# Two chunks in one TensorE group from chunk 6 instead of chunk 8, with every instruction put in order anew

## The chip, the cores and the metric

The program runs on one core of a Trainium2 chip. The core has five engines with queues of their own: TensorE (PE in the profile, with its weight loads apart as PEld), VectorE (DVE), ScalarE (ACT), GpSimd (POOL) and SyncE (SP, which issues most DMAs here). The metric is the device time of one execution in microseconds.

## The reference, cut to what matters

```
for t in range(S):                       # S = 768, B = 4, H = 8, D = 48
    state = alpha[t] * state + outer(k[t], v[t])      # per batch and head, D x D
    y[t]  = q[t] @ state
x = y as B*S tokens of H*D = 384
h = x @ w_in                             # 384 -> 2048, fp64 weights on the host
g = h * tanh(softplus(h))
out = g @ w_out                          # 2048 -> 384
```

A gated linear recurrence ("the attention") runs over 768 steps, and a feed-forward network ("the FFN") is applied to each of the 3072 tokens it gives.

## The kernel before, in words

**Chunks.** The 768 steps are cut into 12 stretches of 64. A chunk is one stretch of two of the four batches with all heads, 128 tokens, so there are 24, numbered 0 to 23; chunk n needs the state that chunk n-2 leaves. For a chunk VectorE makes two scans of the decays (`scan_rest` L672, `scan_front` L685), multiplies k and q by them (L681, L695) and decays the state (L700). TensorE then has three groups of many small matmuls: `turn` (the keys transposed, L724), `front` (what the old state gives, L752, and the scores, L763), and `back` (the scores times v, L790, and the update of the state, L802). Between front and back VectorE masks the scores; after back ScalarE takes the upper half of the fp32 result for x (`upper`, L831) and VectorE the lower half (`lower`, L837), and the state is gathered (L874).

**Two chunks in one group.** From chunk `PAIR_FROM` = 8 on, `attention` takes two chunks (two pairs of batches, same stretch of time) into one turn, one front and one back (L536 to 580). Such a pair borrows both PSUM banks `h` of the FFN for its scores and again for its update, so an FFN unit that would hold a bank then copies it away first (`put_by`, L1041, in units named by `leave_early`). Earlier chunks have their three groups each.

**Options of an unpaired chunk.** `DIRECT` chunks put their last heads straight into place with extra small matmuls (L745, L783); the others write them to a side tile x3, which six small DMAs carry into x (`move`, L858, from SP or, by `MOVER`, from ScalarE's queue). `X_PE` chunks have the lower half made by TensorE (`off`, L844) and ScalarE, with the state's update as a group of its own behind it. `STATE_PE` chunks have the old state added by TensorE (L809) in place of VectorE.

**FFN.** A unit is one of 16 blocks of 128 hidden columns for two or four chunks: nine up matmuls (L1017), seven ScalarE and VectorE steps, and three down matmuls for each chunk (L1089). 100 units run in the order of `SEGMENTS`: first four blocks for chunks 0 and 1, four for 2 and 3, then blocks 4 to 10 for chunks 0 to 3, then (unit 15 on) chunks 4 to 7, and from unit 36 on four chunks at a time. The fp64 weights of a block are loaded (L415), turned into fp32 words by three VectorE steps (L428, L433, L438), and split into an upper half by ScalarE (L449) and a lower half; `W_LOW` says which engine makes that: TensorE (L467, L468 and a copy by ScalarE), GpSimd (L477, two steps) or VectorE (L455).

**Order.** The kernel does not rely on the order of its code: `Plan.add` collects tasks with a cost, a due key, needs and buffers, and `Plan.order` simulates the engines once at build time and writes each engine's queue. Constants such as `LEAD`, `DUE_SHIFT`, `W_SHIFT`, `KEYS`, `COST` and the DMA rates feed that simulation alone. Until the model's time 43, `fill` matmuls without a result (L1165) stand where TensorE would have nothing to do.

Of the kernel before, what the change touches and what calls it, by code (L numbers as in the profile page):

```python
# [39 lines left out]
QKA = 2 * NSEG * L + NSEG * (L + 1) + 1  # L40
# [13 lines left out]
LEAD = 5.5  # L54
SPREAD = 3.0
W_LEAD = 4.25
GATE = -2.0
Q_LEAD = 4.75
V_LEAD = 9.75
FIRST_W = -22.25  # L60
# [40 lines left out]
BEGIN = {"PE": 3.0, "DVE": 4.3, "ACT": 2.2, "POOL": 4.2, "SP": 1.2}  # L101
# [20 lines left out]
class Plan:  # L122
# [26 lines left out]
    def order(self):  # L149
# [51 lines left out]
        while len(done) < n:  # L201
# [49 lines left out]
            if t.size:  # L251
                dma_free = max(at + DMA_FIRST, dma_free) + t.size / DMA_RATE
                t.late = dma_free + DMA_LAST - at
                loads.append(t)
# [20 lines left out]
KEYS = 60.0  # L275
PER_KEY = {'PE': 0.03, 'DVE': 0.02, 'ACT': 0.02, 'POOL': 0.02, 'SP': 0}
# [1186 lines left out]
```

## Time and profile before

| | us |
|---|---|
| three runs, median (lowest to highest) | 499.86 (497.8 to 502.82) |
| profiled execution, its time | 497.71 |
| its span, first to last instruction | 496.0 |
| busy in it: PE, DVE, ACT, POOL | 484.6, 323.1, 382.1, 25.3 |
| mean granted share of TensorE's clock | 0.998 |

A busy PE says that some matmul was under way, so it includes the fills. In the merged rows of a timeline the duration of a group ends with its last matmul's modelled end, which overlaps the next group; what a group costs TensorE is the difference between its start and the start of the next one. On VectorE too the recorded spans overlap a little, so starts are compared where they stand side by side.

### The profile page before, as it was taken

The numbers are of one execution on the slowest core, as the hardware profiler recorded it, in microseconds if no ns is written. First come the engines' busy times: TensorE is split into PE (matmuls) and PEld (weight loads), VectorE is DVE, ScalarE is ACT, GpSimd is POOL, SyncE is SP. The second block draws the span as 40 slices with busy tenths as digits, with TensorE's granted clock in tenths as the row PEclk, the third lists the DMA queues.
The fourth block names the chain that finished last, engine by engine and source line by source line (L and its number), as shares of the span: only waits on it lengthen the run. The fifth ranks groups of instructions, "written<-read, shape, count | busy, mean of one in ns | idle before, by whom it ended". The sixth has DMA issues, their size and how long they took to land.

```text
span 496.0 us, 12822 instructions
## 1 busy us (share of the span) xinstructions
PE 484.6 (98%) x5319; PEld 432.5 (87%) x5319; DVE 323.1 (65%) x522; ACT 382.1 (77%) x864; POOL 25.3 (5%) x27
## 2 busy tenths in 40 slices
PE   6999999999999999999999999999999999999995
PEld 4688889899899989999989899999989899999994
DVE  7999999999973694447867783863474343343333
ACT  3578786886788778857777897889789899997772
POOL 2003201413000000000000000000000000000000
PEclk9999999999999999999999999999999999999999
DMA  7877544606000250115152543603153412100001
GB/s 248 316 285 236 181 151 157 238 35 214 13 0 9 78 172 1 66 59 175 28 213 75 183 164 99 207 24 118 71 171 93 172 41 106 64 1 0 1 0 68
DMA packets 18926, 56.22 MB, mean 113 GB/s; under 512 B 3440, under 2 KB 11312, under 8 KB 18864
## 3 DMA queue, kind: packets, MB, share of 16 engines
q1 hardware_dynamic: 18592, 55.11, 32.5%
q8 instruction: 42, 0.69, 0.6%
q10 hardware_dynamic: 272, 0.26, 0.2%
q14 instruction: 20, 0.16, 0.1%
HBM read 48.87 MB, written 4.72 MB: 108 GB/s over the span
## 4 chain that ended last, share of the span: by engine, by line
PE 85%; DVE 9%; DMA 3%; issue 1%; ACT 1%; SPq 0%; DVEq 0%; ACTq 0%
PE sums_at L1089 39%; PE h_at L1017 37%; PE att_at L790 2%; PE att_at L752 2%; DVE w_lead L433 2%; PE h_at L763 2%; DMA ws<-in_wp_dram 1%; DVE w_lead L438 1%; PE att_at L724 1%; DMA qka<-in_qka_dram 1%; PE h_at L802 1%; DVE w_lead L428 1%; DVE t L1044 1%; DVE g L1054 1%; DVE rest L672 1%
## 5 line engine op out<-in xcount | busy, mean ns | idle before, releaser
L1089 PE MATMUL sums_at<-ws,g 128*128 128x384 f32 x1152 | 223.9, 340 | 0.1
L1017 PE MATMUL h_at<-xs,ws 128*128 128x512 f32 (+1 forms) x900 | 214.2, 384 | 0.2 <-DVE t L1044 0.2
L1089 PEld LDWEIGHTS sums_at<-ws,g 128*128 128x128 f32 x1152 | 202.4, 188 | 8.1 <-ACT ws L471 0.4
L1017 PEld LDWEIGHTS h_at<-xs,ws 128*128 128x128 f32 x900 | 163.3, 188 | 28.4 <-DVE t L1044 0.5
L1054 DVE SCALAR_TENSOR_TENSOR g<-t,g 128x512 fp32r<-128x512 f32 (+1 forms) x100 | 67.8, 679 | 124.2 <-ACT g L1051 123.9
L1026 ACT ACTIVATE t<-h_at 128x512 f32<-128x512 f32 (+1 forms) x100 | 58.0, 580 | 63.6 <-PE h_at L1017 60.8
L1051 ACT ACTIVATE g<-t 128x512 fp32r<-128x512 f32 (+1 forms) x100 | 60.3, 604 | 11.5 <-PE sums_at L1089 5.3
L1029 ACT ACTIVATE t<-t 128x512 f32<-128x512 f32 (+1 forms) x100 | 61.3, 613 | 2.3
L1032 ACT ACTIVATE t<-t 128x512 f32<-128x512 f32 (+1 forms) x100 | 61.2, 612 | 2.2
L1044 DVE SCALAR_TENSOR_TENSOR t<-t,h_at 128x512 f32<-128x512 f32 (+1 forms) x87 | 57.1, 657 | 8.3 <-ACT t L1035 8.2
L1035 ACT ACTIVATE t<-t 128x512 f32<-128x512 f32 (+1 forms) x100 | 60.4, 604 | 0.5
L672 DVE TENSOR_TENSOR_SCAN rest<-qka,behind 112x520 f32<-112x520 f32 x24 | 30.4, 1268 | 0.4 <-DMA qka<-in_qka_dram 0.2
L685 DVE TENSOR_TENSOR_SCAN qka<-qka,ahead 112x520 f32<-112x520 f32 x24 | 30.6, 1274 | 0.0
L477 POOL TENSOR_TENSOR ws<-w_lead,ws 128x384 fp32r<-128x384 f32 x14 | 22.1, 1598 | 98.3 <-ACT ws L449 98.3
L1026 ACT ACTIVATION_READ_ACCUMULATOR t<-h_at 128x1 f32 x100 | 19.4, 194 | 0.0
L1041 DVE COPY held<-h_at 128x512 f32<-128x512 f32 x13 | 9.0, 691 | 15.8 <-ACT t L1026 15.8
L831 ACT ACTIVATE xs<-att_at 112x384 fp32r<-112x384 f32 (+1 forms) x24 | 12.2, 513 | 6.2 <-PE att_at L809 3.4
L695 DVE TENSOR_TENSOR qka<-qka 112x512 f32<-112x512 f32 x24 | 16.4, 684 | 0.1
L681 DVE TENSOR_TENSOR qka<-qka,rest 112x512 f32<-112x512 f32 x24 | 15.8, 659 | 0.0
L433 DVE SCALAR_TENSOR_TENSOR w_lead<-ws,w_lead 128x768 int32<-128x768 int32 x16 | 15.7, 982 | 0.1
L438 DVE SCALAR_TENSOR_TENSOR w_lead<-ws,w_lead 128x768 int32<-128x768 int32 x16 | 15.3, 957 | 0.1
L449 ACT ACTIVATE ws<-w_lead 128x768 fp32r<-128x768 f32 x16 | 13.4, 839 | 2.3 <-DVE w_lead L438 2.2
(100 smaller groups left out, 366.7 us busy)
## 6 DMA issues: line engine op xcount, KB each, us to landing
qka<-in_qka_dram SPq DMA_DIRECT2D x22, 772.5 KB, 5.8
ws<-in_wp_dram SPq DMA_DIRECT2D x16, 768.0 KB, 4.5
wc<-in_wp_dram SPq DMA_DIRECT2D x16, 768.0 KB, 4.5
v<-in_vp_dram SPq DMA_DIRECT2D x24, 192.0 KB, 4.5
out_dram<-osb SPq DMA_DIRECT2D x15, 192.0 KB, 2.6
xs<-x SPq DMA_DIRECT2D x104, 16.0 KB, 1.8
out_dram<-part SPq DMA_DIRECT2D x8, 192.0 KB, 2.6
qka<-in_qka_dram SPq DMA_DIRECT2D x2, 260.5 KB, 4.4
```

Source lines behind the costliest of these rows:

```text
L433: nc.vector.scalar_tensor_tensor(lead.tile, words(1), -0x40000000, lead.tile, ALU.bitwise_and, ALU.bitwise_or)
L672: nc.vector.tensor_tensor_scan(t[:, :0:-1], alpha()[:, :0:-1], behind[:, ::-1], 0.0, ALU.mult, ALU.max)
L685: nc.vector.tensor_tensor_scan(a, a, ahead, 0.0, ALU.mult, ALU.max)
L1017: nc.tensor.matmul(p[:, :N].rearrange("p (c t) -> p c t", c=nt), wi[:, z, f, s], x[:, :, s, a], start=m == 0, stop=m == len(passes) - 1,)
L1026: nc.scalar.activation(wide(t), wide(h), AF.Exp, accum_out=vchk[:, at : at + 1])
L1029: nc.scalar.activation(wide(t), wide(t), AF.Square, bias=1.0)
L1032: nc.scalar.activation(wide(t), wide(t), AF.Ln, bias=0.2, scale=0.2)
L1035: nc.scalar.activation(wide(t), wide(t), AF.Exp, scale=-1.0)
L1044: nc.vector.scalar_tensor_tensor(wide(y), wide(t), 2.5, wide(held), ALU.subtract, ALU.mult)
L1051: nc.scalar.activation(g.tile[:, 0, :N], wide(y), AF.Copy, scale=-0.4, accum_out=own)
L1054: nc.vector.scalar_tensor_tensor(g.tile[:, 1, :N], wide(y), -0.4, g.tile[:, 0, :N].bitcast(F32), ALU.mult, ALU.subtract,)
L1089: nc.tensor.matmul(o.tile, g.tile[:, a, j * C : (j + 1) * C], wo[:, z, f], start=begins and m == 0, stop=end and m == 2,)
```

## The change

`PAIR_FROM` goes from 8 to 6, so chunks 6 and 7 become a pair. Beside it nearly all constants of the order are new, and some of them choose other engines: `DIRECT` loses chunks 0, 6 and 7; `X_PE` goes from {0, 1} to chunks 1 to 5 (its higher entries name paired chunks and do nothing); `STATE_PE` goes from {2, 6} to 3, 4 and 5 (6 and 7 do nothing); `W_LOW` no longer uses GpSimd: blocks 4, 7, 8, 11, 12, 13 and 15 go to VectorE, and blocks 0 and 2 use the banks `h`. The weights of the six blocks in `PARTS` are loaded and converted in two halves. One cast at the start (L333) is gone, and the last output goes out by SP's queue. The model's costs and DMA rates are new as well.

```diff
-LEAD = 5.5
+LEAD = 5.75
...
-W_LEAD = 4.25
+W_LEAD = 6.75
...
-Q_LEAD = 4.75
-V_LEAD = 9.75
-FIRST_W = -22.25
+Q_LEAD = 6.5
+V_LEAD = 6.75
+FIRST_W = -20.25
...
 DUE_SHIFT = {
-    0: -3.75, 1: 1.75, 2: 2.5, 3: 1.0, 4: -1.5, 5: 2.0, 6: 2.0, 7: 2.0, 8: -4.5, 9: -6.5, 10: -11.25,
...
+    0: -5.25, 1: -5.5, 2: -4.5, 3: 1.75, 4: -1.0, 5: -0.5, 6: -3.25, 7: 4.5, 8: -1.0, 9: -7.75,
...
-X_PE = {0, 1}
+X_PE = {1, 2, 3, 4, 5, 6, 7, 8, 9}
 SIDES = 2
-STATE_PE = {2, 6}
-PAIR_FROM = 8
+STATE_PE = {3, 4, 5, 6, 7}
+PAIR_FROM = 6
 BACK_AFTER = 0.8
-DIRECT = {0, 1, 2, 3, 6, 7}
+DIRECT = {1, 2, 3}
 W_LOW = {
-    0: ('PE', 'o0'), 1: ('PE', 'o0'), 2: ('PE', 'o3'), 3: ('PE', 'o3'), 4: ('POOL', ''), 5: ('PE', 'o0'),
-    6: ('DVE', ''), 7: ('POOL', ''), 8: ('POOL', ''), 9: ('DVE', ''), 10: ('DVE', ''), 11: ('POOL', ''),
-    12: ('POOL', ''), 13: ('POOL', ''), 14: ('DVE', ''), 15: ('POOL', ''),
+    0: ('PE', 'h'), 1: ('PE', 'o0'), 2: ('PE', 'h'), 3: ('PE', 'o0'), 4: ('DVE', ''), 5: ('PE', 'o3'),
+    6: ('DVE', ''), 7: ('DVE', ''), 8: ('DVE', ''), 9: ('DVE', ''), 10: ('DVE', ''), 11: ('DVE', ''),
+    12: ('DVE', ''), 13: ('DVE', ''), 14: ('DVE', ''), 15: ('DVE', ''),
 }
...
+PARTS = {7, 8, 10, 12, 14, 15}
+OUT_LATER = 4.0
...
-FLIGHT = 1800.0
+FLIGHT = 2200.0
...
-DMA_RATE, DMA_FIRST, DMA_LAST = 285.0, 1.1, 0.9
+DMA_RATE, DMA_FIRST, DMA_LAST, DMA_EACH = 355.0, 1.7, 0.8, 0.1
+DMA_SLOW, DMA_SLOW_UNTIL = 0.3, 22.0
...
-KEYS = 60.0
-PER_KEY = {'PE': 0.03, 'DVE': 0.02, 'ACT': 0.02, 'POOL': 0.02, 'SP': 0}
+KEYS = 80.0
+PER_KEY = {'PE': 0.02, 'DVE': 0.05, 'ACT': 0.02, 'POOL': 0.08, 'SP': 0.01}
...
-    causal_f = sb.tile([P, L], F32, tag="rest", name="causal_f", bufs=BUFS["rest"])
+    causal_f = const.tile([P, L], F32, name="causal_f")
...
-    causal = const.tile([P, L], U32, name="causal")
-    nc.vector.tensor_copy(causal, causal_f)
-    causal8 = causal.unsqueeze(1).unsqueeze(1).broadcast_to([P, 2, NPAIR, L])
+    causal8 = causal_f.bitcast(U32).unsqueeze(1).unsqueeze(1).broadcast_to([P, 2, NPAIR, L])
...
     def weight(f):
         key = weight_unit[f] - W_LEAD + W_SHIFT.get(f, 0.0)
+        if f not in PARTS:
+            weight_part(f, slice(0, 2), key, "")
+            return
+        for m in range(2):
+            weight_part(f, slice(m, m + 1), key + m * OUT_LATER, "1")
+
+    def weight_part(f, which, key, part):
         stage = plan.buffer("stage")
+        size = which.stop - which.start
...
-                queue = nc.scalar if n == n_chunks - 1 else nc.sync
-                queue.dma_start(by_token[c * L : (c + 1) * L, 2 * b : 2 * b + 2], osb.tile)
+                nc.sync.dma_start(by_token[c * L : (c + 1) * L, 2 * b : 2 * b + 2], osb.tile)
```

## Rows read from the trace of the kernel before

**Rows 1.** The page's first part: busy time, share of the span and instructions.
```profile
PE 484.6 (98%) x5319; PEld 432.5 (87%) x5319; DVE 323.1 (65%) x522; ACT 382.1 (77%) x864; POOL 25.3 (5%) x27
```
**Rows 2.** Windows: stretch, PE, PEld, DVE, ACT, POOL busy, clock, DMA share, GB/s.
```profile
0.00:23.00 23.00, 17.55 (x277) 12.72 (x278) 19.80 (x31) 8.71 (x21) 3.25 (x13) 1.00 0.80 273
...
45.00:92.00 47.00, 46.99 (x778) 41.69 (x778) 46.15 (x74) 36.23 (x88) 10.82 (x7) 1.00 0.54 190
```
**Rows 3.** The first window for the fills of L1165 alone (PE, PEld).
```profile
0.00:23.00 23.00, 9.80 (x29) 5.92 (x29) 1.00 0.80 273
```
**Rows 4.** Timeline of PE, chunk 6 (unpaired): start us, us, line, count.
```profile
70.28 0.58 PE L745 MATMUL att_at<-qka,v_apart 48*64 48x64 f32 x24
...
71.59 2.35 PE L1089 MATMUL sums_at<-ws,g 128*128 128x384 f32 x12
73.87 0.58 PE L783 MATMUL att_at<-probs,v_apart 64*64 64x64 f32 x24
...
75.07 0.90 PE L809 MATMUL att_at<-state,ident 112*112 112x192 f32 x4
75.68 2.36 PE L1017 MATMUL h_at<-xs,ws 128*128 128x512 f32 x9
```
**Rows 5.** Timeline of PE, the pair of chunks 8 and 9.
```profile
112.87 0.69 PE L752 MATMUL att_at<-qka,state 48*64 48x64 f32 x32
...
114.89 1.33 PE L1089 MATMUL sums_at<-ws,g 128*128 128x384 f32 x6
...
118.11 2.26 PE L1089 MATMUL sums_at<-ws,g 128*128 128x384 f32 x12
120.29 0.69 PE L790 MATMUL att_at<-probs,v 64*64 64x64 f32 x32
...
122.11 1.33 PE L1089 MATMUL sums_at<-ws,g 128*128 128x384 f32 x6
```
**Rows 6.** The chain that ended last: start us, us; twelve downs between ups.
```profile
105.85 2.12 PE sums_at L1089 x12
```
**Rows 7.** Timeline of PE, chunk 0's lower half (`off`) and the next group.
```profile
14.35 0.51 PE L844 MATMUL att_at<-xs,minus_ident 128*128 128x192 f32 x2
14.68 0.57 PE L724 MATMUL sums_at<-ident,qka 112*128 112x112 f32 x4
```
**Rows 8.** Timelines of DVE and PE where unit 15 begins.
```profile
90.72 0.56 DVE L837 TENSOR_TENSOR xs<-att_at,xs 128x384 fp32r<-128x384 f32 x1
91.19 0.56 DVE L874 TENSOR_TENSOR state<-att_at,state 112x384 f32<-112x384 f32 x1
...
91.64 2.24 PE L1017 MATMUL h_at<-xs,ws 128*128 128x512 f32 x9
```
**Rows 9.** Line L428 until 91.2 us: count, ns min/median/max, first and last start.
```profile
L428 DVE TENSOR_SCALAR w_lead<-ws x12: 545/552/562, 8.7 to 85.8; 128x768 int32<-128x768 int32 x12
```
**Rows 10.** Groups of VectorE by line and shape: busy us, mean ns | idle before.
```profile
L433 DVE SCALAR_TENSOR_TENSOR w_lead<-ws,w_lead 128x768 int32<-128x768 int32 x16 | 15.7, 982 | 0.1
...
L1041 DVE COPY held<-h_at 128x512 f32<-128x512 f32 x13 | 9.0, 691 | 15.8 <-ACT t L1026 15.8
L837 DVE TENSOR_TENSOR x<-att_at,x 112x128 fp32r<-112x128 f32 x18 | 5.1, 283 | 1.5 <-ACT xs L831 1.4
L455 DVE TENSOR_TENSOR ws<-w_lead,ws 128x768 fp32r<-128x768 f32 x4 | 3.8, 954 | 0.0
```
**Rows 11.** Lines L477 (GpSimd) and L685 (a scan): ns min/median/max.
```profile
L477 POOL TENSOR_TENSOR ws<-w_lead,ws x14: 1012/1184/4257, 45.0 to 123.3; 128x384 fp32r<-128x384 f32 x14
L685 DVE TENSOR_TENSOR_SCAN qka<-qka,ahead x24: 1226/1233/2056, 5.7 to 370.7; 112x520 f32<-112x520 f32 x24
```
**Rows 12.** DMA issues: count, KB each, median us to landing; L858's issue ns.
```profile
out_dram<-osb SPq DMA_DIRECT2D x15, 192.0 KB, 2.6
xs<-x SPq DMA_DIRECT2D x104, 16.0 KB, 1.8
...
out_dram<-osb ACTq DMA_DIRECT2D x1, 192.0 KB, 3.2
...
L858 SPq DMA_DIRECT2D xs<-x x104: 507/587/1611, 51.3 to 406.0; - x104
```

More of the change, by code (lines that the diff above doesn't have):

```diff
@@ L251, in order @@
             if t.size:
-                dma_free = max(at + DMA_FIRST, dma_free) + t.size / DMA_RATE
+                dma_free = max(at + DMA_FIRST, dma_free) + t.size / DMA_RATE + DMA_EACH
+                dma_free += DMA_SLOW * (2.0 < at < DMA_SLOW_UNTIL and t.size > 300)
                 t.late = dma_free + DMA_LAST - at
@@ L410, in weight @@
         key = weight_unit[f] - W_LEAD + W_SHIFT.get(f, 0.0)
+        if f not in PARTS:
[4 more added lines that the diff above has]
+    def weight_part(f, which, key, part):
         stage = plan.buffer("stage")
+        size = which.stop - which.start
         def load():
-            t = new(stage, [P, 2, DM, 2], f"ws{f}", dtype=I32)
+            t = new(stage, [P, size, DM, 2], f"ws{f}", dtype=I32)
             return nc.sync.dma_start(
                 t.rearrange("p m c w -> p (m c w)"),
-                w[f].rearrange("p m c -> p (m c)").bitcast(I32),
+                w[f, :, which].rearrange("p m c -> p (m c)").bitcast(I32),
             )
-        got = add(
-            "SP", *COST["load"], max(key, FIRST_W + f) - 4, load, uses=[stage], size=786
-        )
+        first = max(key, FIRST_W + f) - 4
+        got = add("SP", *COST["load"], first, load, uses=[stage], size=393 * size)
         lead = plan.buffer("lead")
@@ L426, in begin @@
         def begin():
-            new(lead, [P, 2, DM], f"w_lead{f}", dtype=I32)
+            new(lead, [P, size, DM], f"w_lead{f}", dtype=I32)
             nc.vector.tensor_scalar(
@@ L455, in lower @@
                 nc.vector.tensor_tensor(lo, both(), hi.bitcast(F32), ALU.subtract)
-            b = add("DVE", *COST["w lo2"], key + 0.035, lower, [a], [lead], port=True)
-            ready_w[f, 0] = ready_w[f, 1] = [a, b]
+            b = add("DVE", *COST[f"w lo{size}"], key + 0.035, lower, [a], [lead], port=True)
+            for m in range(which.start, which.stop):
+                ready_w[f, m] = [a, b]
             return
-        for m in range(2):
+        for m in range(size):
             k = key + 0.5 * m
@@ L481, in weight @@
                 b = add("POOL", *COST["w lo"], k + 0.04, lower, [a], [lead], port=True)
-            ready_w[f, m] = [a, b]
+            ready_w[f, which.start + m] = [a, b]
     def weight_check(f):
@@ L654, in chunk @@
             got_a, got_k, got_q = (
-                add("SP", *COST["load"], -99 + 0.1 * i, load_part(*e), uses=[q_buf], size=230)
+                add("SP", *COST["load"], -99 + 0.1 * i, load_part(*e), uses=[q_buf], size=263)
                 for i, e in enumerate(((a_at, QKA), (k_at, a_at), (0, k_at)))
@@ L665, in chunk @@
             got_a = got_k = got_q = add(
-                "SP", *COST["load"], key - Q_LEAD, load, uses=[q_buf], size=692
+                "SP", *COST["load"], key - Q_LEAD, load, uses=[q_buf], size=791
             )
@@ L1064, in unit @@
         t_exp = add("ACT", *cost("exp"), k, exp, [t_up], [h, t])
-        t_sq = add("ACT", *cost("act"), k + 0.01, square, [t_exp], [t])
+        t_sq = add("ACT", *cost("square"), k + 0.01, square, [t_exp], [t])
         t_ln = add("ACT", *cost("ln"), k + 0.02, log, [t_sq], [t])
@@ L1151, in send @@
                 b, c = chunks[n]
[L1152 to L1153 removed]
+                nc.sync.dma_start(by_token[c * L : (c + 1) * L, 2 * b : 2 * b + 2], osb.tile)
             copied = add("ACT" if on_act else "DVE", *COST["stash"], k, copy, done, [o, osb])
[L1156 to L1157 removed]
+            add("SP", *COST["store"], k + 0.001, send, [copied], [osb])
     if FILLS:
```

57 lines of the change are left out of this document (29 added, 28 removed), and 4 rows, old and new, of the table DUE_SHIFT.

## The prediction, made before the changed kernel was seen running

> **What bounds the kernel now.** I read the busy times first. TensorE has work under way for 98% of the span, VectorE for 65% [rows 1]. That is an average over stages, so I cut the span into windows. In the first 23 us TensorE is busy for 17.55, but 9.80 of that are fills, which compute nothing [rows 2, 3]. Real work is therefore 17.55 - 9.80 = 7.75 us, and 15.25 us of TensorE's time are lost before the first FFN unit has got going. From 45 to 92 us TensorE has no gap at all (46.99 of 47) and VectorE hardly one (46.15 of 47) [rows 2]. So two engines are full there at once: VectorE prepares chunks and weights, and TensorE uses them up as they come. How tight this is shows at unit 15, the first that needs chunks 4 to 7: the lower half of chunk 7's x starts on VectorE at 90.72, the next instruction there starts at 91.19, and the unit's first up matmul starts at 91.64 [rows 8]. After that the chain of waits is TensorE's own work, ups and twelve downs in turn (2.12 us a set of downs [rows 6]), up to the end.
>
> So the end is: TensorE's total work, plus what it loses before unit 15, plus a short tail. The change can act through these three alone, and all chunks and blocks it touches before unit 15 must also pass VectorE, which has no room. After unit 15 the work is the same in both kernels.
>
> **TensorE's work, part by part.** All durations are differences of starts.
>
> Pairing chunks 6 and 7. Unpaired, chunk 6 has a front of 71.59 - 70.28 = 1.31, and a back with update and state of 75.68 - 73.87 = 1.81, of which the state on TensorE (L809) is 75.68 - 75.07 = 0.61 [rows 4]. Chunk 7 is the same without the state, 1.31 + 1.20. Together 5.63. The pair of 8 and 9 has a front of 114.89 - 112.87 = 2.02 and a back of 122.11 - 120.29 = 1.82, together 3.84 [rows 5]. The turns have as many matmuls either way; I count them at nothing. That is -1.79. A group of small matmuls also slows the FFN group beside it: twelve downs take 2.12 undisturbed [rows 6], 73.87 - 71.59 = 2.28 between a front and a back [rows 4], and 120.29 - 118.11 = 2.18 with one such neighbour [rows 5], so some 0.08 a border. Three groups fewer are six borders, -0.47. Sum -2.3.
>
> Lower halves on TensorE. Chunk 0's `off` takes 14.68 - 14.35 = 0.33 [rows 7]. Chunks 2 and 3 gain one each. Chunks 4 and 5, which are not direct, have twice as many matmuls in it: no row shows that, so between 0.33 and 0.66; I take 0.5, since the added ones are narrower. In each of the four the update becomes a group of its own, two borders or 0.16. Together 0.66 + 1.0 + 0.64 = +2.3. Chunk 0 loses its `off` and the extra group, -0.5, and by not being direct about 0.3 more, the difference per chunk between chunk 6's back without the state (1.20) and half of the pair's (0.91) [rows 4, 5].
>
> State on TensorE. Chunks 3, 4 and 5 in place of 2 (chunk 6 is counted above): two more at 0.61 [rows 4], +1.2.
>
> The five blocks whose lower weights TensorE makes stay five. Sum: -2.3 + 2.3 - 0.8 + 1.2 = **+0.4 us**. What the pair saves on TensorE is spent on taking work from VectorE.
>
> **VectorE before unit 15.** Removed: the large x step, 0.47 by the start of its neighbour [rows 8], for chunks 2 and 3, and that with the small one (0.28 [rows 10]) for 4 and 5: -2.4. State additions, of the same size as the large x step: three go, those of chunks 2 and 6 come, -0.5. Added: both x steps for chunk 0, +0.75; the small step for 6 and 7, +0.6; one or two copies that clear the borrowed banks, 0.69 each at most [rows 10], +1.1; lower weights of blocks 4, 7 and 8, 0.95 each [rows 10], +2.8. Halving the steps of blocks 7, 8 and 10: not in the trace; from nothing up to 0.1 for each of twelve steps that become two, I take +0.7. Given back by GpSimd: one scan took 2.06 against a median of 1.23 [rows 11]; the others that met GpSimd's steps before unit 15 lost little, so -1.0. The removed cast gives nothing, as VectorE is idle for 3.2 of the first 23 us anyway [rows 2], most of it before data is there. Sum **+2.1 us**. The cover: until 91.2 VectorE had begun 12 blocks' conversions [rows 9], and only eleven are needed before unit 25. The twelfth can wait, 0.55 + two times 0.98 or 2.5 us [rows 9, 10]. So I cost VectorE's surplus at nothing; without that cover unit 15 comes up to 2.1 us later.
>
> Here the Trainium skill speaks for more. SBUF — State Buffer, "Who interferes with whom", says that VectorE with two SBUF inputs and GpSimd reading SBUF share one read interface, and that the second "fully blocks" until the first is done. By that page all 10.82 us of GpSimd's work from 45 to 92 [rows 2] could stand in VectorE's way, and the sum would be lower by up to 9. The scan's one doubling agrees with the page; the near-full VectorE and median steps of usual length do not show such a loss, so I keep 1.0.
>
> **The moves.** Chunks 0, 6 and 7 now send six small DMAs each. An issue takes 0.59 us and a landing 1.8 [rows 12]. Chunk 0's are hidden behind chunk 1's scans. Those of 6 and 7 stand between the pair's last x step and unit 15, where before the x step alone did: for one chunk's six on one queue 6 x 0.59 + 1.8 = 5.3 us. They hide if the pair is done that much earlier, under the downs of the units before; its due keys are earlier. Bounds 0 and 5.3; I take 0.5, because TensorE in that stretch still has units of blocks 8 to 10 to do, but no reserve beyond [rows 2]. SP's loads stand behind these moves; DMA is at 0.54 there, which is room.
>
> **The start and the tail.** What the new order does in the first 23 us no row shows. The supplier, VectorE, is idle for 23 - 19.80 = 3.2 us [rows 2], so -3.2 is as far as a fuller start goes, and I take the same for a load that comes late. Value -0.5. The last store lands in 2.6 us from SP where ScalarE's queue took 3.2 [rows 12]: between 0 and -0.6, value -0.3.
>
> **Sum.** +0.4 + 0 + 0.5 - 0.5 - 0.3 = +0.1 against the profiled execution's 497.71, or 497.8. That execution is 2.15 below the median of the runs (499.86), so the same sum against the median is 500.0. I put the forecast between them, **498.9 us**.
>
> **Rivals.**
> A, the start closes. The loads are due in another order, and GpSimd no longer touches VectorE. For it: 15.25 us lost, the largest loss there is. Against: unit 15 waits for VectorE, whose work does not shrink, so TensorE would only wait later. With -3.2 and another -2 from VectorE meeting no GpSimd: 498.9 - 5.2 = 493.7. The lock that the Trainium skill describes would act through this case.
> B, unit 15 waits, slower than before. The pair needs both chunks scanned, masked and moved, and borrows both `h` banks while VectorE is full; VectorE's +2.1 is uncovered and 3 of the 5.3 us of moves show. 498.9 + 5.1 = 504.0. It decides once the pair's last move lands after the downs of units 12 to 14 have run out.
> C, the pairing does nothing that shows: TensorE's +0.4 without the six borders (+0.47): 499.4.
>
> **How the numbers follow.** A measurement of this kernel tells about 1% (5 us) from no change. Forecast 0.60, A 0.15, B 0.15, C 0.10. A and B lie across the 1% bound with two thirds to three quarters of their weight: faster 0.11, same 0.77, slower 0.12. The range takes in the forecast's terms (-3.2 at the start, +2.1 and more at unit 15), the 2 us between runs and part of A and B: 494.5 to 503.5.
>
> **What would show it.** Chunks 6 and 7 as one front of about 2.0 and one back of about 1.8 us; no row of GpSimd at L477's successor; scans near 1.23 throughout; unit 15 within 3 us of 91.64; fills and gaps before 23 us between 12 and 18 us; no TensorE wait after unit 15. The prediction is wrong if unit 15 starts before 88 or after 95, or if a new wait of TensorE on VectorE or on a move appears between 60 and 100 us.

## The result, and the profile after

The changed kernel takes 505.9 us (median of 4 runs, 505.04 to 506.23) against 499.62 of the kernel before on the same chip (4 runs, 497.8 to 502.82). The ratio is **1.0139, 95% interval 1.0111 to 1.0166**: slower by 1.4%, and outside the range given. The profiled execution took 505.04 us with a span of 503.3; before it was 497.71 and 496.0, so 7.3 us are to be found.

The page of the changed kernel, first part; it answers to [rows 1]:

```profile
PE 491.3 (98%) x5267; PEld 437.2 (87%) x5267; DVE 328.0 (65%) x552; ACT 386.1 (77%) x874; POOL 3.2 (1%) x13
```

TensorE is busy for 6.7 us more, fills included, with 52 matmuls fewer. The share of the span, 98%, says nothing of it. The windows do (stretch, PE, PEld, DVE, ACT, POOL busy, clock, DMA share, GB/s); the first and the last answer to [rows 2]:

```profile
0.00:23.00 23.00, 19.64 (x261) 13.85 (x261) 18.64 (x31) 7.72 (x20) 3.21 (x13) 1.00 0.73 237
23.00:45.00 22.00, 21.03 (x403) 16.63 (x403) 21.04 (x33) 15.46 (x43) 0.00 (x0) 1.00 0.80 272
45.00:92.00 47.00, 46.96 (x726) 41.60 (x725) 44.94 (x82) 35.33 (x87) 0.00 (x0) 1.00 0.56 181
```

The second stretch of the kernel before, which [rows 2] leaves out:

```profile
23.00:45.00 22.00, 21.89 (x416) 17.82 (x414) 21.97 (x37) 17.16 (x47) 0.00 (x0) 1.00 0.76 275
```

From 45 to 92 us TensorE has no gap, as before. Ahead of 45 us its busy time holds more fills. The window from 0 to 45 us for the fills alone, first of the kernel before, then of the changed one (PE, PEld):

```profile
0.00:45.00 45.00, 10.50 (x31) 6.22 (x31) 1.00 0.78 274
```

```profile
0.00:45.00 45.00, 15.61 (x45) 9.29 (x45) 1.00 0.77 254
```

So 5.1 us more of TensorE's time there compute nothing. Fills and gaps together go from 15.25 to 16.11 us in the first 23 us, and from 0.81 to 3.83 us between 23 and 45. A ledger of TensorE's time up to the first matmul of unit 15, by differences of starts, makes this exact; here is the first matmul of unit 15 in the changed kernel, beside the one in [rows 8]:

```profile
97.33 0.86 PE L1030 MATMUL h_at<-xs,ws 128*128 128x512 f32 x3
```

| until unit 15 starts | before | changed | difference |
|---|---|---|---|
| fills | 9.90 | 14.75 | +4.85 |
| gaps | 2.73 | 1.47 | -1.26 |
| work that counts | 76.17 | 78.21 | +2.04 |
| before the first matmul | 2.85 | 2.89 | +0.04 |
| unit 15 starts at | 91.64 | 97.33 | +5.69 |

From unit 15 to unit 36 another 1.06 us are lost (97.02 against 98.08), from 36 to 99 nothing (291.20 against 291.19), and from unit 99 to the span's end 0.56 (16.14 against 16.70). 5.69 + 1.06 - 0.01 + 0.56 = 7.30.

The 1.06 us have one place. VectorE of the changed kernel, and TensorE beside it (start us, us, engine, line; in brackets the idle time before and its releaser):

```profile
184.70 1.24 DVE L685 TENSOR_TENSOR_SCAN rest<-qka,behind 112x520 f32<-112x520 f32 x1 [2.06 <-DMA qka<-in_qka_dram]
...
186.66 1.23 DVE L698 TENSOR_TENSOR_SCAN qka<-qka,ahead 112x520 f32<-112x520 f32 x1
187.81 0.66 DVE L1057 SCALAR_TENSOR_TENSOR t<-t,h_at 128x512 f32<-128x512 f32 x1
...
188.53 1.21 PE L1030 MATMUL h_at<-xs,ws 128*128 128x512 f32 x4 [1.31 <-DVE t L1057]
```

Chunk 13's load lands late, its scans stand in VectorE's queue, and the gate (L1057) that gives an h bank back to TensorE stands behind them.

What the prediction said of single steps shows up. The pair of chunks 6 and 7 on TensorE, the answer to [rows 5]: front 78.44 - 76.42 = 2.02, back 85.64 - 83.83 = 1.81 us.

```profile
76.42 0.69 PE L765 MATMUL att_at<-qka,state 48*64 48x64 f32 x32
...
78.44 1.32 PE L1102 MATMUL sums_at<-ws,g 128*128 128x384 f32 x6
...
83.83 0.69 PE L803 MATMUL att_at<-probs,v 64*64 64x64 f32 x32
...
85.64 0.63 PE L1102 MATMUL sums_at<-ws,g 128*128 128x384 f32 x2
```

And the scans, where [rows 11] had one of 2.06 us (ns min/median/max):

```profile
L698 DVE TENSOR_TENSOR_SCAN qka<-qka,ahead x24: 1215/1234/1237, 5.7 to 389.5; 112x520 f32<-112x520 f32 x24
```

### The profile page after: what moved, and what is told of

Its sections match the earlier page's. It is cut to its first block, busy times and chain, and to the rows that moved or that the text cites. A ratio compares the mean times of both kernels' runs of the same rounds, so it can differ in the third digit from the quotient of the medians.

```text
span 503.3 us, 12781 instructions
## 1 busy us (share of the span) xinstructions
PE 491.3 (98%) x5267; PEld 437.2 (87%) x5267; DVE 328.0 (65%) x552; ACT 386.1 (77%) x874; POOL 3.2 (1%) x13
## 4 chain that ended last, share of the span: by engine, by line
PE 89%; DVE 5%; DMA 4%; issue 1%; ACT 0%; SPq 0%; DVEq 0%
PE sums_at L1102 40%; PE h_at L1030 38%; DMA ws<-in_wp_dram 3%; PE att_at L765 2%; PE att_at L803 2%; PE h_at L776 2%; PE att_at L737 1%; DMA qka<-in_qka_dram 1%; PE h_at L815 1%; DVE qka L698 1%; DVE w_lead L444 1%; DVE rest L685 1%; PE sums_at L480 1%; PE att_at L822 0%; DVE w_lead L449 0%
## 5 line engine op out<-in xcount | busy, mean ns | idle before, releaser
L1057 DVE SCALAR_TENSOR_TENSOR t<-t,h_at 128x512 f32<-128x512 f32 (+1 forms) x84 | 55.0, 654 | 9.8 <-ACT t L1048 9.6
L685 DVE TENSOR_TENSOR_SCAN rest<-qka,behind 112x520 f32<-112x520 f32 x24 | 29.7, 1236 | 3.8 <-DMA qka<-in_qka_dram 3.6
L461 ACT ACTIVATE ws<-w_lead 128x384 fp32r<-128x384 f32 (+1 forms) x22 | 14.6, 662 | 9.0 <-DVE w_lead L449 8.9
L1054 DVE COPY held<-h_at 128x512 f32<-128x512 f32 x16 | 11.0, 689 | 14.3 <-ACT t L1039 14.2
L1176 PE MATMUL sums_at<-minus_ident 128*128 128x512 f32 x45 | 15.6, 474 | 2.9 <-ACT minus_ident L340 2.9
L449 DVE SCALAR_TENSOR_TENSOR w_lead<-ws,w_lead 128x384 int32<-128x384 int32 (+1 forms) x22 | 16.0, 733 | 0.2
L444 DVE SCALAR_TENSOR_TENSOR w_lead<-ws,w_lead 128x384 int32<-128x384 int32 (+1 forms) x22 | 16.0, 734 | 0.2
L803 PEld LDWEIGHTS att_at<-probs,v 64*48 64x48 f32 (+1 forms) x744 | 13.0, 126 | 3.1 <-issue 1.8
L803 PE MATMUL att_at<-probs,v 64*48 64x64 f32 (+1 forms) x744 | 15.7, 220 | 0.0
## 6 DMA issues: line engine op xcount, KB each, us to landing
qka<-in_qka_dram SPq DMA_DIRECT2D x22, 772.5 KB, 5.4
```

Of the source, the lines that this page charges most:

```text
L685: nc.vector.tensor_tensor_scan(t[:, :0:-1], alpha()[:, :0:-1], behind[:, ::-1], 0.0, ALU.mult, ALU.max)
L803: nc.tensor.matmul(y[64 * a : 64 * a + wide, u, j], V()[own, h : h + wide], probs[slot][own, a, j], start=first and j == 0 and not direct ...
L1057: nc.vector.scalar_tensor_tensor(wide(y), wide(t), 2.5, wide(held), ALU.subtract, ALU.mult)
```

## The experiments

After the result I held **theory S**: the new order gives VectorE and TensorE their work ahead of 45 us so that TensorE runs short, and the rest is TensorE's own extra work. Rivals were late loads (L), VectorE's amount of work ahead of unit 15 (V), and pairing itself (P). All kernels keep the order of every queue unless it says otherwise; each ratio is to the kernel before, timed beside it. When a unit's first up matmul starts, in the profiled executions (us):

| kernel | unit 0 | unit 3 | unit 8 | unit 15 | unit 36 | unit 97 | span | ratio (95%) |
|---|---|---|---|---|---|---|---|---|
| before | 22.72 | 40.87 | 55.32 | 91.64 | 188.66 | 471.52 | 496.0 | 1 |
| changed | 29.81 | 41.95 | 63.27 | 97.33 | 195.41 | 478.25 | 503.3 | 1.0139 (1.0111 to 1.0166) |
| e1 | 29.82 | 41.02 | 62.37 | 96.40 | 193.89 | 476.70 | 501.8 | 1.0106 (1.0088 to 1.0124) |
| e2 | 29.62 | 41.10 | 62.35 | 96.41 | 194.43 | 477.23 | 502.2 | 1.0116 (1.0101 to 1.0131) |
| e3 | 29.25 | 40.69 | 62.47 | 96.54 | 198.19 | 481.04 | 505.5 | 1.0202 (1.0183 to 1.0220) |
| e4 | 28.71 | 40.16 | 61.48 | 95.55 | 194.20 | 477.00 | 501.9 | 1.0112 (1.0086 to 1.0138) |
| e5 | 28.78 | 40.77 | 62.60 | 96.60 | 194.86 | 477.70 | 502.7 | 1.0148 (1.0128 to 1.0168) |
| e6 | 30.20 | 41.42 | 62.76 | 96.81 | 193.88 | 476.69 | 501.8 | 1.0071 (1.0051 to 1.0091) |
| g1 | 29.49 | 40.54 | 61.86 | 96.11 | 194.18 | 477.01 | 502.0 | 1.0100 (1.0073 to 1.0126) |
| g2 | 28.96 | 40.14 | 62.15 | 96.91 | 194.54 | 477.35 | 502.5 | 1.0136 (1.0109 to 1.0163) |
| k1 | 29.58 | 40.77 | 62.16 | 95.58 | 193.94 | 476.75 | 501.8 | 1.0093 (1.0072 to 1.0114) |
| j1 | 23.74 | 41.85 | 63.17 | 97.24 | 195.42 | 478.28 | 503.6 | 1.0111 (1.0090 to 1.0131) |
| h1 | 29.23 | 41.53 | 63.18 | 97.21 | 194.70 | 477.50 | 503.0 | 1.0131 (1.0110 to 1.0152) |
| h2 | 29.68 | 41.98 | 63.62 | 98.26 | 195.79 | 478.62 | 503.3 | 1.0125 (1.0105 to 1.0145) |
| h3 | 29.91 | 42.22 | 63.86 | 97.93 | 195.43 | 478.26 | 502.9 | 1.0126 (1.0108 to 1.0143) |
| b1 | 22.61 | 41.61 | 57.04 | 93.36 | 190.36 | 473.22 | 497.7 | 1.0042 (1.0025 to 1.0058) |
| f1 | 29.78 | 40.42 | 61.31 | 95.82 | 192.19 | 474.68 | 499.6 | 1.0097 (1.0072 to 1.0122) |
| f2 | 31.21 | 40.87 | 60.56 | 100.70 | 197.99 | 480.16 | 505.8 | 1.0193 (1.0170 to 1.0216) |
| f3 | 28.38 | 41.18 | 59.23 | 97.97 | 194.55 | 476.19 | 502.3 | 1.0150 (1.0108 to 1.0193) |
| f5 | 28.66 | 39.48 | 60.08 | 99.36 | 196.21 | 478.40 | 503.9 | 1.0131 (1.0105 to 1.0157) |

The changed kernel, e3, e4 and e6 are the same up to unit 32, and their unit 15 starts at 97.33, 96.54, 95.55 and 96.81. So 1.8 us at unit 15 between single profiles is no effect. The spread stands ahead of unit 3 (40.16 to 41.95); loads land at different times there, and block 0's conversion begins at 9.2, 8.6, 8.1 and 9.6 us. The time from unit 3 to unit 15 tells more: it is 55.38 to 55.40 us in the changed kernel, e1, e4, e6 and j1 (55.85 in e3). The ratios have the intervals beside them; two of them less than some 0.0035 apart can't be told from each other.

**Are the loads late? e1.**

```diff
-            if t.paced:
+            if False and t.paced:
```

> The changed kernel with the rule 'few loads in flight' taken out: every load is issued as soon as its buffer is free; order of all queues kept. Changed kernel for comparison: 505.04 us profiled, ratio 1.0139 to the kernel before. Theory S (the start's order: TensorE loses about 3 us more than before ahead of 45 us because VectorE and TensorE are given work in an order that leaves TensorE short, and the loads are only a part of it): between -1.0 and +0.5 us against the changed kernel, unit 0 still after 28 us. Rival L (late loads: blocks and chunks land too late because only two loads may be in flight): -2 to -4 us, unit 0 before 27 us and the waits of VectorE for blocks at 9.2 and 33.6 us gone.

Unit 0 starts at 29.82 and unit 15 at 96.40, within that spread. VectorE still waits for block 0's load at 9.2 us (1.16 us). Only the wait at 187 us shrinks, from 1.31 to 0.8. Theory L falls for the start.

**Does TensorE's extra work set unit 15? e2 and e5.** e2 adds the states of chunks 3 to 5 on VectorE, e5 makes the lower halves of chunks 2 to 5 there.

```diff
+STATE_DVE = {3, 4, 5}                                  # e2
-            if on_pe:
+            if on_pe and n not in STATE_DVE:           # in update, and so in gather
...
+LOWER_DVE = {2, 3, 4, 5}                               # e5: off issues nothing,
+                    nc.vector.tensor_tensor(to(1), of, to(0).bitcast(F32), ALU.subtract)   # left does this
```

> The changed kernel with the states of chunks 3, 4 and 5 added by VectorE as for most chunks before, in place of two matmuls each and a copy by ScalarE; order kept. Takes 3 x 0.61 = 1.83 us off TensorE from 44.7 us on, gives VectorE three steps of about 0.55. Theory S (from 45 us on TensorE's own work sets the time and VectorE has cover): -1.2 to -1.9 us against the changed kernel, that is 503.2 to 503.8. Rival V (the prediction's view, unit 15 waits for VectorE, which has no room): 0 to +1.6 us, unit 15 later than 97.3 us or a TensorE wait ahead of it.

> The changed kernel with the lower halves of x of chunks 2, 3, 4 and 5 made by VectorE, in place of matmuls and a copy by ScalarE; order kept. Takes 0.33 + 0.33 + 0.56 + 0.51 us off TensorE (the first two ahead of 45 us, where it is short of work anyway), gives VectorE four steps of 0.47 and two of 0.28, +2.4 us. Theory S (TensorE's own work sets the time from 45 us on, VectorE has cover): -0.7 to -1.7 us against the changed kernel. Rival V (VectorE without room sets unit 15): +0.5 to +2.4 us, with TensorE waiting for VectorE between 45 and 97 us.

Neither theory has its way: unit 15 starts at 96.41 and 96.60, as without the edits, and 55.31 and 55.83 us after unit 3. In e2 the first place where the saving is lost is a new wait of TensorE for the state that VectorE now adds:

```profile
44.84 0.55 DVE L888 TENSOR_TENSOR state<-att_at,state 112x384 f32<-112x384 f32 x1
...
45.45 0.60 PE L738 MATMUL att_at<-ident,qka 112*128 112x112 f32 x4 [0.80 <-DVE state L888]
```

So e2 could not tell whether TensorE's stream sets unit 15, since it put a step with a wait in place of what it took. k1 takes the same matmuls out and puts nothing there.

```diff
+STATE_OUT = {3, 4, 5}
-            if on_pe:
+            if on_pe and n not in STATE_OUT:
```

> The changed kernel with the two matmuls that add the old state left out for chunks 3, 4 and 5 and nothing put in their place (this part of the computation is missing; every other instruction and the order of all queues stay). It takes 3 x 0.61 = 1.83 us off TensorE, as e2 did, but without e2's new step on VectorE for which the next turn had to wait. Theory T (from 45 us on TensorE's own stream sets the time; e2 lost its gain to the wait on VectorE that it brought): unit 15 at 94.6 to 95.2 us where e1, e3 and e6 had 96.4 to 96.8, time -1.5 to -1.8 us against the changed kernel. Rival Q (something that no experiment has touched sets unit 15): 96.2 or later, time unchanged.

Unit 15 starts at 95.58, which is within the spread of the kernels with the same start (e4: 95.55), and the ratio, 1.0093, has an interval that overlaps the changed kernel's. Counted from unit 3 it comes after 54.81 us in place of 55.38 to 55.40, so 0.57 of the 1.83 us arrive; expected were 1.5 to 1.8. From unit 8 to unit 15 the 0.61 us of chunk 5's group arrive in full (33.43 against 34.04 to 34.07). Ahead of unit 8 the two other groups bring nothing (21.38 from unit 3 to unit 8, against 21.32 to 21.34): a front (L766) now waits 0.5 us at 46.7 us for ScalarE's copy of the turned keys. So theory T holds in part: TensorE's stream sets the time from unit 8 to unit 15, and ahead of that other waits stand close behind it.

**Does VectorE's amount of work set it? g1 and g2.** g1 gives the lower weights of blocks 4 and 6 to 10 to GpSimd again; g2 adds e2 and half of e5.

```diff
+LOW_POOL = {4, 6, 7, 8, 9, 10}
+                if f in LOW_POOL:
+                    for m in range(size):
+                        nc.gpsimd.tensor_tensor(
+                            lo[:, m], both()[:, m], hi[:, m].bitcast(F32), ALU.subtract
+                        )
+                    return
                 nc.vector.tensor_tensor(lo, both(), hi.bitcast(F32), ALU.subtract)
```

> The changed kernel with the lower weights of blocks 4 and 6 to 10 made by GpSimd, half a block at a time, as the kernel before did for four of them; order of all queues kept. Takes some 5 us off VectorE ahead of unit 15 and nothing off TensorE. Theory V (VectorE's work ahead of unit 15 alone sets its start): unit 15 at 92 to 94 us in place of 96.4 to 97.3, time -2 to -4 us against the changed kernel. Theory T (TensorE's own work alone sets it from 45 us on, as it has no gap there): unit 15 within 0.5 us of 96.5, time unchanged. Theory B (both engines are loaded to the same level there, and one relieved alone leaves the other): as T here, but g2 gains.

> g1, and besides the states of chunks 3 to 5 and the lower halves of x of chunks 4 and 5 on VectorE in place of TensorE: both engines relieved at once (VectorE by 5 less 3.1 us, TensorE by 1.83 + 1.07 = 2.9). Theory B: unit 15 at 94 to 95 us, time -1.5 to -2.9 us against the changed kernel, where e2 and e5 (TensorE relieved alone) left unit 15 at 96.4 and 96.6. Theory V: no better than g1. If unit 15 stays at 96.4 here too, neither engine's amount of work but a chain between them sets it (the two h banks that the pair borrows, the queue order).

The windows of g1:

```profile
0.00:23.00 23.00, 19.54 (x261) 13.93 (x261) 19.12 (x31) 7.99 (x20) 3.21 (x13) 1.00 0.73 243
23.00:45.00 22.00, 21.95 (x409) 17.65 (x410) 21.90 (x35) 16.24 (x44) 0.00 (x0) 1.00 0.77 270
45.00:97.00 52.00, 52.00 (x749) 45.90 (x748) 47.92 (x82) 40.36 (x98) 15.12 (x11) 1.00 0.53 174
```

VectorE has 4.1 us of slack from 45 to 97 us, TensorE none, and unit 15 starts at 96.11, 55.57 us after unit 3. Theory V falls: unit 15 does not wait for VectorE's amount of work. g2 gains nothing either (96.91); TensorE waits there 3.8 us in three places for states that VectorE adds, more than in e2.

**Is it unit 0's late start? j1.** Block 2's lower weights use bank o3, so that unit 0 need not wait for an h bank.

```diff
-    0: ('PE', 'h'), 1: ('PE', 'o0'), 2: ('PE', 'h'), 3: ('PE', 'o0'), ...
+    0: ('PE', 'h'), 1: ('PE', 'o0'), 2: ('PE', 'o3'), 3: ('PE', 'o0'), ...
```

> The changed kernel with block 2's lower weights worked out in bank o3 instead of an h bank; every task keeps its place in the order but for unit 0, which no longer waits for block 2 to give the h bank back. Asked: is it unit 0's late start (29.8 us against 22.7) that costs the time ahead of 45 us? If it is: units 0 to 15 all come earlier, unit 15 by 1 us or more, and fills fall by as much. If TensorE's supply as a whole is short there (blocks and chunks that come late from VectorE): unit 0 at 23 to 25 us, units 3 to 15 within 0.5 us of where they were, fewer fills early and as many more later, time within 0.5 us of the changed kernel.

```profile
23.74 1.31 PE L1198 MATMUL h_at<-xs,ws 128*128 128x256 f32 x9
...
97.24 1.09 PE L1198 MATMUL h_at<-xs,ws 128*128 128x512 f32 x4
```

Unit 0 comes 6.1 us earlier, unit 3 0.1, unit 15 0.1. The most visible difference between the two starts is a symptom: the place in TensorE's queue that unit 0 leaves is not filled by anything that comes earlier too.

**Is it the order of chunks and blocks on VectorE? h1, h2 and b1.** Up to 45 us VectorE spends 21.7 us on chunks (scans, multiplications, decays) and 16.2 on blocks' conversions before, and 22.9 and 13.8 in the changed kernel. TensorE has begun five units before (a sixth at 44.99) and four after. h1 puts two scans behind two blocks in the changed kernel, h2 does so without the rule on loads, b1 puts two scans ahead of two blocks in the kernel before.

```diff
+    behind_of(nth("chunk.<locals>.scan_rest", 4), nth("weight_part.<locals>.ends", 3))   # h1, h2
+    behind_of(nth("chunk.<locals>.scan_rest", 5), nth("weight_part.<locals>.ends", 5))
...
+    ahead_of(nth("chunk.<locals>.scan_rest", 4), nth("weight.<locals>.signs", 3))        # b1
+    ahead_of(nth("chunk.<locals>.scan_rest", 5), nth("weight.<locals>.begin", 5))
```

> The changed kernel with two steps of VectorE moved and nothing else: the first scan of chunk 4 (31.05 us) to behind block 3's conversion (it ends at 36.5), the first scan of chunk 5 (41.4 us) to behind the conversion of the sixth block (46.9), so that blocks come ahead of chunks as in the kernel before. Theory S (TensorE runs short ahead of 45 us because VectorE makes chunks ready before the blocks that the first units need): the block's conversion can begin only when its load has landed (33.4 us), so VectorE waits there and most of the gain is lost: unit 3 within 0.5 us of 41.0, unit 15 within 0.7 of 96.5, time -0.5 to +0.5. Rival (the queue order alone is enough): unit 3 before 40.2, time -1 or more.

> h1, and the rule 'few loads in flight' taken out as in e1, so that block 3's load is issued 2.4 us earlier. Theory S: now unit 3 at 39.5 to 40.3 us (e1 without the move: 41.02), fills and gaps ahead of unit 15 some 1 us less than in e1, unit 15 at 95.2 to 95.9 (e1: 96.40), time -0.5 to -1.2 us against e1 (1.0106). If unit 15 stays at 96.4 although unit 3 comes earlier, TensorE's short supply ahead of 45 us is not in these two scans.

> The kernel before with the opposite edit and nothing else: on VectorE the first scan of chunk 4 (33.5 us) goes ahead of two of the three steps of the block converted at 30.8 to 33.1 us, and the first scan of chunk 5 (45.7) ahead of the block begun at 40.9. Their loads have landed by then. Theory S: blocks come 1.2 us later, units 3 and 4 about 1.2 us later than 40.87 and 42.46, more fills ahead of 45 us, and 0.8 to 2 us more in all (ratio 1.0015 to 1.004). Rival (TensorE's supply there does not hang on the order of chunks and blocks): ratio within 0.001 of 1.

b1 has the size that theory S expects: the split up to 45 us becomes 22.9 and 14.7, units 3, 5 and 8 start 0.7, 1.2 and 1.7 us later, unit 15 at 93.36, and the ratio is 1.0042 (2.1 us). The way there is another. The moved scan stands between two steps of a block, but ahead of the lower half of chunk 2's x (L837) too:

```profile
30.78 1.24 DVE L672 TENSOR_TENSOR_SCAN rest<-qka,behind 112x520 f32<-112x520 f32 x1
31.94 0.93 DVE L433 SCALAR_TENSOR_TENSOR w_lead<-ws,w_lead 128x768 int32<-128x768 int32 x1
32.79 0.55 DVE L837 TENSOR_TENSOR xs<-att_at,xs 128x384 fp32r<-128x384 f32 x1
```

ScalarE's copy of the state waits for that step, and chunk 3's turn on TensorE waits for the copy (who waits for whom, us in total, times, longest):

```profile
PE att_at L724 <- ACT state L872: 1.0, 1, 1.0
```

Up to unit 15 gaps grow by 1.15 us and fills by 0.10. So b1 shows what the places of two steps on VectorE are worth; that it is late blocks that leave TensorE short, it does not show.

The same edit the other way round does not give it back. h1 is as expected, at the edge of its bounds; h2 misses: unit 3 at 41.98, not 39.5 to 40.3. In h2 block 3's conversion ends 1.2 us earlier than in the changed kernel, but its second half on TensorE (L480) comes at the old time, since it needs a bank that ScalarE's copy (L484) gives free, and ScalarE stands ahead of that copy for a check (L702) that reads chunk 4's scan:

```profile
38.45 0.31 ACT L702 ACTIVATE chk<-qka,minus 112x8 f32<-112x8 f32 x1 [1.38 <-DVE qka L698]
...
38.97 0.47 ACT L484 ACTIVATE ws<-sums_at 128x384 fp32r<-128x384 f32 x1
...
39.49 0.91 PE L480 MATMUL sums_at<-w_lead,ident 128*128 128x384 f32 x2 [1.25 <-ACT ws L484]
```

One order is thus built into three queues, and one queue put right alone hands the wait to the next.

**The wait at 187 us and the tail: e3, e4, e6, h3.** e3 moves five steps of chunk 13 behind unit 32's gate and lower half, e6 its second scan alone behind the gate; both send the last store from ScalarE's queue.

```diff
+    tasks.remove(scan)                                  # e6: chunk 13's scan_front
+    tasks.insert(tasks.index(nth("unit.<locals>.gate", 32)) + 1, scan)
...
+                queue = nc.scalar if n == n_chunks - 1 else nc.sync
```

> The changed kernel with two late edits: the last store goes out on ScalarE's queue as before, and VectorE's five steps that scan chunk 13 stand behind the gate and the lower half of g of unit 32 and not ahead of them (the scans wait for chunk 13's load, and the gate stood behind them while TensorE waited 1.3 us for it at 187 us). If both places are worth what the trace shows: -0.65 at the tail and -1.3 at 187 us, together about -2.0 us against the changed kernel, unit 36 at about 194.1 in place of 195.41. Rival (the wait comes back some units later, since VectorE has the same work to do behind a late load): -0.6 us only, with a new wait between 187 and 230 us.

> The changed kernel with the last store on ScalarE's queue (the tail was 0.6 us shorter so in e3) and, on VectorE, the gate of unit 32 ahead of the second scan of chunk 13 instead of behind it, and nothing else moved. e3 moved too much behind the load: the gate of unit 33 then stood behind five steps and TensorE waited 3.4 us. If the place of one step of 1.2 us decides: unit 36 at 1.0 to 1.2 us less than in the changed kernel for the same unit 15, the wait at 187 us under 0.3, in all -1.7 us. Rival (the late load only moves the wait to the next gate): -0.6 us from the tail alone.

> What e4 was meant to be: the last store on ScalarE's queue, and on VectorE the second scan of chunk 13 just behind the gate of unit 32 instead of ahead of it. In e4 the gate was put ahead of the step that makes its input, so its values were not the right ones and its wait was not the real one. If the place of this one step decides the wait at 187 us: unit 36 less unit 15 about 97.0 us in place of 98.1, and with the tail -1.7 us against the changed kernel. Rival (the late load only moves the wait on): -0.6 us from the tail alone.

e3 is a miss, and its ratio, 1.0202, is the slowest of all. The gate of unit 33 now stands behind the five steps and a decay, 4.3 us of VectorE's work in a row, and TensorE waits 3.40 us for it:

```profile
192.46 3.80 PE L1030 MATMUL h_at<-xs,ws 128*128 128x512 f32 x9 [3.40 <-DVE t L1057]
```

The nine ups behind the wait take 3.80 us, where nine took 2.24 at 186.28: from 192 to 194 us TensorE's granted clock is 0.55 on average, down from 1.00. So of the 3.6 us that e3 loses against the changed kernel between units 15 and 36, 2.1 are the longer wait and some 1.5 the clock. e4 put the gate ahead of the step that makes its input, so its time from there on (1.0112 in all) tells nothing. e6 has the gate at 185.34 and the wait down to 0.29:

```profile
185.34 0.69 DVE L1057 SCALAR_TENSOR_TENSOR t<-t,h_at 128x512 f32<-128x512 f32 x1 [0.34 <-ACT t L1048]
185.94 1.23 DVE L698 TENSOR_TENSOR_SCAN qka<-qka,ahead 112x520 f32<-112x520 f32 x1
...
189.63 2.32 PE L1030 MATMUL h_at<-xs,ws 128*128 128x512 f32 x9 [0.29 <-DVE t L1057]
```

Unit 36 less unit 15 is 97.07 us as expected (97.0). With 1.0071, e6 is the fastest of the changed family. Of the 3.4 us (with an uncertainty of 1.7) between the two ratios, its profile shows 1.0 by the place of one 1.2-us step; 0.5 stand ahead of unit 15, within the spread, and the rest is not in it. The tail is less clear: from TensorE's last end to the span's end it takes 5.7, 5.9, 6.1 and 6.3 us in the four of these kernels that use ScalarE's queue, 6.0 to 6.8 in those that don't.

> The changed kernel with every edit that helped: no rule on loads in flight (e1), the two scans behind the blocks (h2), the second scan of chunk 13 behind the gate of unit 32 and the last store on ScalarE's queue (e6: ratio 1.0071). If the places add up: e6 less 0.5 to 1.5 us, ratio 1.004 to 1.006, still slower than the kernel before because the start keeps most of its loss and TensorE its 2 us more of work ahead of unit 15.

h3 doesn't add up: 1.0126, because the h2 part costs more than the rest gives.

**Order against choices: f1, f2, f3, f5.** These have the due keys of single chunks, blocks and units shifted by a search of the same kind and length, with the costs of the kernel before in the planner. f1 has the changed kernel's engines and pairs; f5 (f2 mended) the same engines with pairs from 8; f3 the engines of before with pairs from 6.

```diff
+BEGINS = [-99.0000, ...]        # one due key for each task, in place of the constants' keys
+LEAVE = [10, 11, 20, ...]       # the units that copy their bank away
-PAIR_FROM = 6                   # f5 alone
+PAIR_FROM = 8
```

> The changed kernel, same engine choices and same pairs from chunk 6 on, but the order of all instructions found once more: the planner is given the durations that the kernel before used, and the due keys of single chunks, blocks and units were shifted until its plan was 2.4 us shorter than the plan of the changed kernel's own order by the same durations (496.9 against 499.3). Theory S (what was lost is in the order, above all ahead of 45 us): about -2.4 us against the changed kernel, ratio 1.007 to 1.010 to the kernel before. Rival V (VectorE's work ahead of unit 15 sets the time, and the order can't take it away): within 1 us of the changed kernel, ratio 1.012 to 1.016.

> The same as f1 with one difference in the engine choices: chunks 6 and 7 stay apart and pairs begin at chunk 8, as before; the order found anew with as many trials. If pairing 6 and 7 gives TensorE the 2.3 us that the prediction counted: about +2 us against f1 (its plan says 498.9 against 496.9). Rival P (the pair costs as much as it saves, since both chunks must be scanned at once and both h banks are lent while units 12 to 14 want them): within 1 us of f1, or faster than f1.

> The engine choices of the kernel before (lower weights of seven blocks on GpSimd, lower halves of chunks 2 to 5 on VectorE, states of chunk 2 alone) with pairs from chunk 6 on, the order found anew with as many trials: the pairing alone. If pairing is what made the kernel slower: ratio 1.010 or more to the kernel before, as the changed kernel. If pairing is worth its 2.3 us of TensorE and the other choices were what cost time: ratio 0.994 to 1.000. Its plan says 498.4, against 494.9 for the kernel before: a ratio of 1.007, because VectorE has no room for both chunks ahead of the pair's front.

> f2 once more, with an order in which chunk 0's state is read before chunk 1's update writes into the same bank (in f2 it was read behind it, so f2's states were not the reference's). Engine choices of the changed kernel, chunks 6 and 7 apart, pairs from 8 on, order found anew with at least as many trials as f1. If the pair of 6 and 7 is worth TensorE's 2.3 us: 1.5 to 3 us more than f1 (its plan is 1.8 longer). Rival P (the pair gives nothing): within 1 us of f1, ratio 1.008 to 1.012.

f1 is 1.0097 against 1.0139, about 2.1 us with an uncertainty of 1.9, with the same instructions on the same engines. In its profile the gain is not at the start: unit 15 is at 95.82, and fills and gaps ahead of it are 15.1 us, both as in e4. It comes behind, with 96.37 us from unit 15 to unit 36 in place of 98.08. So f1 speaks for the order as a cause, as far as an order found by a short search can, but not for the start. f3 is 1.0150: pairing 6 and 7, with an order found anew, makes the kernel before as slow as the changed one, where TensorE's saving should have made it faster. f5 less f1 is 0.0034, or 1.7 us with an uncertainty of 1.8. This is not the pair alone: in f5 chunks 6 and 7, no longer paired, also have their lower halves and states made by TensorE, since `X_PE` and `STATE_PE` name them (five state groups ahead of unit 15, three in f1). So what the pair itself is worth stays open. f2 gave 1.0193, with chunk 0's state read too late. TensorE's fills and gaps up to unit 15 are 12.6 us before, 13.7 in f5 and 15.9 in f2, all with pairs from 8, and 15.1, 16.2 and 18.2 in f1, the changed kernel and f3, the three with pairs from 6.

## Why the prediction was wrong

**Where it was right.** The pair takes 2.02 and 1.81 us. VectorE's work up to unit 15 grows from 87.6 to 89.6 us, +2.0 where +2.1 was worked out; in part by luck, since it now holds one block less and 3.6 us of chunk 8's steps, neither of them in the sum. Scans take 1.23 throughout. The moves of chunks 6 and 7 hold nothing up: the last one lands at 95.97 us, and TensorE has no gap up to unit 15. And VectorE's extra work is covered, as costed: g1 relieves VectorE and unit 15 stays. The cover was another one than named, though. Only eleven blocks are converted ahead of unit 15, but the time went to chunk 8's steps; what covers VectorE is that TensorE had fallen behind.

**The step that failed** is "The start and the tail": "Value -0.5", with bounds of 3.2 either way taken from VectorE's idle time in the first 23 us. Fills and gaps ahead of unit 15 grew by 3.6 us in this profile (2.5 to 3.8 in the four with the same start), and the prediction's own sign of being wrong, unit 15 after 95 us, came. Two things were wrong in the bound. It looked at the first 23 us alone: there fills and gaps were 16.1 us, within the 12 to 18 that it gave, and most of the loss, 3.0 us, came between 23 and 45 us, where the kernel before loses only 0.8. And it took the supplier's idle time for what a new order can change. VectorE's idle time from its first step up to 45 us did grow, from 2.3 to 4.4 us, but what VectorE makes in its busy time changed as well: 2.4 us less of blocks and 1.2 more of chunks. b1 shows that two scans of 1.2 us each in the wrong place cost 1.7 us at unit 15 and 2.1 in all, with VectorE's idle time as before, in a kernel that is otherwise the one before. Since TensorE has no gap from 45 us to unit 15 in either kernel, what is lost ahead of it is never made good. That a chunk scanned early gave TensorE nothing to do while a unit lacked its block is how theory S reads this; no run shows it.

**Mis-sized terms.** TensorE's work was put at +0.4 and is +2.0 up to unit 15 in that profile, +1.4 in e6 (0.5 of the difference is in the turns of chunks 0 and 3). The x and weight `off` groups came as costed (+1.34 against 1.33), the pair too. The border terms of the sum (-0.47 for the pair, +0.64 for four updates of their own, about -0.16 for chunk 0's) cancel, and ups and downs together do cost the same as before (43.9 us). What the sum did not have: the backs of chunks 2 to 5, now without the update behind them, take 0.1 us longer each, and the turns take 0.2 us more in e6, 0.7 in the changed kernel. The tail was put at -0.3 and is +0.56.

**"No TensorE wait after unit 15"** was wrong by the 1.3 us at 187 us. The prediction had looked for late loads up to unit 15 alone; the new order also shifts them where three q and k buffers are shared by two pairs.

**The rivals.** The time lies near rival B's 504.0, but not by its mechanism: no unit from 45 to 100 us waits for the pair's moves or for VectorE, and unit 15 is late mostly because TensorE was behind at 45 us. Rival A's cause, the start, was the right place with the wrong sign. The Trainium skill's SBUF — State Buffer, "Who interferes with whom", which rival A leaned on, is borne out by g1, with 15.12 us of GpSimd work from 45 to 97 us (ns min/median/max):

```profile
L692 DVE TENSOR_TENSOR_SCAN rest<-qka,behind x24: 1224/1234/2053, 3.7 to 386.3; 112x520 f32<-112x520 f32 x24
L705 DVE TENSOR_TENSOR_SCAN qka<-qka,ahead x24: 1217/1234/1235, 5.6 to 388.2; 112x520 f32<-112x520 f32 x24
```

```profile
L470 POOL TENSOR_TENSOR ws<-w_lead,ws x12: 1016/1185/2527, 47.0 to 97.7; 128x384 fp32r<-128x384 f32 x12
```

One scan of 48 takes 2.05 us instead of 1.23, and a GpSimd step up to 2.53 instead of 1.18. It is not scans alone: six steps of VectorE that meet a GpSimd step, all with two inputs in SBUF, take 0.1 to 0.8 us longer than others of their kind, 3.8 us in all. So of some 5 us that g1 takes off VectorE only 1.7 come back (49.6 to 47.9 us busy from 45 to 97). In the kernel before, the steps stretched like this from 45 to 92 us make some 1.4 us, near the sum's 1.0; the 9 us are not in it.

**What stays open.** What makes the start's loss is not shown. It is not the pacing of loads, not unit 0, not VectorE's amount of work, and f1's new order leaves it (15.1 us of fills and gaps, as in e4). Every order with pairs from 6 had more fills (13.7 to 14.8 us) than those with pairs from 8 (9.9 to 12.0). That fits one reading: the pair's front needs both chunks scanned at once, which brings scans ahead of blocks. It is argued from a few orders of a short search, and f1 speaks against it, since VectorE spends as much on chunks up to 45 us there as before (21.7 us). A longer search might do better for the changed kernel. No kernel run here beats the one before.

## What to carry to other kernels

When an order is made anew, the largest unknown is the stage in which the busiest engine is not yet fed; its price is not bounded by the supplier's idle time (b1 leaves that as it was and costs 2.1 us), and its sign should be taken as open with several microseconds either way. An experiment that takes work off an engine must not put a step with a wait in its place, or it measures the wait (e2 against k1). In queues that run in order, a step is worth what stands behind it: the same scan moved by one place gave 1.0071, moved with four others 1.0202, and part of that is the clock, which fell after the wait of 3.40 us. And single profiles of kernels with the same start differed by 1.8 us at unit 15; the time between two units told effects of 0.6 us apart.

## What the runs showed of the hardware

Loads landed later in places than their median. On the page a q, k and alpha load of 772.5 KB takes 5.4 us from issue to landing in the changed kernel; the two of 165 to 187 us took 6.8 in the median, and the 768 KB that VectorE waited for at 33.59 us had been issued at 26.70. Without the rule on loads in flight (e1) that one was issued at 24.25, yet the fills ahead of unit 15 stayed (14.1 us against 14.0 to 14.75). TensorE's granted clock was 1.00, the upper of its two levels, in the windows shown here, so none of their differences is the clock's. e3 is the exception: after TensorE had waited 3.40 us, the granted clock was 0.55 from 192 to 194 us. Where VectorE and GpSimd met in g1, both were stretched: six VectorE steps by 3.8 us in all, and five of twelve GpSimd steps took 1.6 to 2.5 us in place of 1.0 to 1.2.
